# Turning the unit maxima in a fused attention and dense block: a TensorE product against VectorE block transposes

## The chip, the cores and the metric

One Trainium2 chip, one of its cores. A core has five engines that run side by side, each through its own queue in order: TensorE (PE in the profile, its weight loads PEld), VectorE (DVE), ScalarE (ACT), GpSimd (POOL) and SyncE (SP), which here only issues DMAs. The metric is the device time of one launch in microseconds; a comparison takes the median over several runs.

## What is computed

`x` is 2048 rows of 512 numbers, all float32. The result is `x + s * g`:

```python
xn = _layernorm(x, axis=-1)
# s: attention with 32 heads of 16 channels over the 2048 rows
q, k, v = split(xn @ wqkv)
scores = einsum("bhqd,bhkd->bhqk", q, k) * (16 ** -0.5)
s = einsum("bhqk,bhkd->bhqd", softmax(scores), v).reshape(B, S, D) @ wo
# g: a dense block
g = silu(gelu(xn @ w1 + b1) @ w2 + b2)
out = x + s * g
```

For the softmax the kernel takes the largest score of every query row and head away ahead of the exponential. That maximum has to be known before the exponentials of that row start, so the kernel computes the scores twice: once with the queries along the partitions, to take the maximum, and once with the keys along the partitions, for the exponentials.

## The kernel before

**Units.** The attention is cut into 32 units: unit `u` is a group of 4 heads (`u // 4`) and a chunk of 512 queries (`u % 4`). Products in nearly full precision are made from a high and a low part of each operand (float32r, "hi" and "lo").

**Two stages.** In the first, up to about 470 us of the span, TensorE works through the dense block (`mm`, line 583: products of half the array's height, 64 rows, which run two at a time, one on each row tile, `a` = 0 or 1). Between them `fill` (line 561) puts score products for the maxima, one for each 5 products of the dense block (`APART`), 576 in all, which is units 0 to 8. In the second stage, the loop over `n` at line 976 runs 512 steps. Each step has four transposed score products with their exponentials (`t_one`, line 708: TensorE, then ScalarE), the four products with the values (`pv_step`, line 775, the row of line 781) and three score products for the maxima of units further ahead (`s_op`, line 209). The order inside a step is written out by hand (`ORDER`, `AFTER`).

**Banks.** Results of TensorE go to PSUM banks. In stage one the score products for the maxima take turns on two banks (`s_tile`: `ps_a`, `ps_b`), in stage two on three (`ps_x` joins). The transposed scores take turns on four banks (`t_tile`, line 700: `ps_m` and three of `ps_t`). A product waits until the reader of the bank's earlier content is done.

**Maxima of a unit.** `s_max` (line 188) reduces every score product on VectorE, 512 columns to two maxima (line 191, 2048 times). When the 64 products of a unit are done:

- `s_end0` (line 238): VectorE reduces what is left to 16 columns, negated, `nm` (line 248); GpSimd rounds it to a high part and takes the low part (lines 251 and 252) into `nmh`. Queries lie along the partitions, 128 at a time; the 16 columns are 4 heads by 4 query blocks.
- The second score product wants each head's maxima as two rows along the queries (high and low), which are multiplied with rows of ones. So the columns have to be turned into rows. Units 0 to 27 go through this in pairs, the last four one by one (`units_of`).
- `s_end1` (line 265), some products later: one TensorE product of `nmh` (up to 64 columns) with the identity `ident_r`. Its bank is one of the score ring in stage one, one of the four of `t_tile` in stage two, and one of the score ring for the last unit. In `fill` it takes the slot of a score product (line 565 to 570).
- `s_end2` (line 271): the bank is copied to `mh`, by ScalarE in stage one (line 276) and by VectorE in stage two (line 278), and one DMA on SP stores it to `mh_d` in HBM, rows of 128 numbers (line 279).
- `load_mh` (line 150): two DMAs on SP read `mh_d` into rows 48 and 49, and 112 and 113, of the queries of `t_one` (`QT`), at steps fixed ahead of time.

SP's queue is in order and holds also the loads of queries (line 136), of weights (line 292) and the moves of results (lines 801 to 814).

Of the kernel before, what the change touches and what calls it, by code (L numbers as in the profile page):

```python
# [8 lines left out]
F32 = mybir.dt.float32  # L9
F32R = mybir.dt.float32r  # L10
AF = mybir.ActivationFunctionType
OP = mybir.AluOpType
AX = mybir.AxisListType
# [3 lines left out]
P = 128  # L17
# [6 lines left out]
CH = 512  # L24
NCH = S // CH
F = 1376
FT = (F + P - 1) // P
GH = 4
NG = H // GH
# [7 lines left out]
FILL0 = 30  # L37
APART = 5
# [12 lines left out]
def fused(ctx: ExitStack, tc: tile.TileContext, x, wqk, wv, wo, w1, b1, w2, b2, out):  # L51
    nc = tc.nc
    ctx.enter_context(tc.manual_schedule())
    dpool = ctx.enter_context(tc.tile_pool(name="scratch", bufs=1, space=DRAM))
    keep = ctx.enter_context(tc.tile_pool(name="keep", bufs=1))
# [9 lines left out]
    ones_d = dpool.tile([2, S], F32, name="ones_d")  # L65
    g_d = dpool.tile([S, D], F32, name="g_d")
    den_d = dpool.tile([NG * NCH, GH, CH], F32, name="den_d")
    mh_d = dpool.tile([NG * NCH, 2, GH, CH], F32, name="mh_d")

    ident_r = keep.tile([P, P], F32R, name="ident_r")  # L70
    mhw = keep.tile([1, 1], F32, name="mhw")
    vsb = keep.tile([P, NT, H * VW + DH], F32, name="vsb")
    kts, kws, qts, qzs = [], [], [], []
# [10 lines left out]
            if then:  # L84
                then()

    QS, QT, MX, NM, MH = {}, {}, {}, {}, {}
    SYNC = mybir.DependencyInfo(mybir.DependencyClass.Sync, mybir.DependencyReason.DATA)
    qss = []
    NU = NG * NCH  # L90
# [3 lines left out]
    def s_tile(held=False):  # L94
        pool = s_ring.pop(0)
        if not held:
            s_ring.append(pool)
        return pool.tile([P, CH], F32, name="ps"), pool
# [22 lines left out]
    def new_k(pool):  # L121
        both = pool.tile([P, 2, S], F32R, name=f"kt{len(kts)}")
        kws.append(both)
        kts.append([both[:, p] for p in range(2)])
# [13 lines left out]
    def load_qs(u, sides=range(2)):  # L138
        if u < NU:
            QS[u] = qzs[u % 2] if u < LEAD // 16 else qss[0][:, u % 2]  # L140
            q_rows(QS[u], u, sides)

    def ask_qs(u):
        errands[:0] = [(load_qs, u, (a,)) for a in range(2)]
# [5 lines left out]
    def load_mh(u):  # L150
        assert u in sent
        for a in range(2):
            nc.sync.dma_start(QT[u][64 * a + 48:64 * a + 50].bitcast(F32), mh_d[u, :, a::2, :])

    heads = [(u, st, p) for u in range(NU) for st in range(NCH * NCH) for p in range(2)]
    made = [0, 0]
    done = {u: 0 for u in range(NU)}
    later, ended, errands, sent = [], [], [], set()

    def units_of(u):  # L160
        return (u,) if u >= PAIRED else (u - u % 2, u - u % 2 + 1)

    def tick():
        for e in later:
            e[0] -= 1

    def flush():
        while later and later[0][0] <= 0:
            u = later.pop(0)[1]
            run_off()  # L170
            s_end1(u)
            s_end2(u)

    def at_of(job):
        u, st, p = job
# [27 lines left out]
    def s_one(a):  # L203
        made[a] += 1
        s_whole(heads[made[a] - 1], a)
# [28 lines left out]
    def run_off():  # L234
        while put_off:
            put_off.pop(0)()

    def s_end0(u):
        ended.remove(u)
        nm = qring.tile([P, GH * NCH], F32, name="nm")  # L240
        n = len(units_of(u))
        if u == units_of(u)[0]:
            NM[u] = qring.tile([P, 2, 2, GH * NCH], F32R, name="nmh")[:, :n]
        hl = NM[units_of(u)[0]][:, u % n]
        if u == units_of(u)[-1]:
            later.append([12 if "seen" in prog else 8, units_of(u)[0]])
        mx = MX.pop(u).rearrange("p a b c n -> p (a b) (c n)")
        nc.vector.tensor_reduce(nm, mx, axis=AX.X, op=OP.max, negate=True)  # L248

        def two():  # L250
            nc.gpsimd.tensor_copy(hl[:, 0], nm)  # L251
            nc.gpsimd.tensor_sub(hl[:, 1], nm, hl[:, 0].bitcast(F32))

        put_off.append(two)
        if "seen" in prog or u == NU - 1:
            run_off()
        del QS[u]
        if "seen" in prog:
            ask_qs(u + 2)
        else:  # L260
            load_qs(u + 2)

    prog = {}

    def s_end1(u):
        pm = s_tile()[0] if "seen" in prog or u == NU - 1 else t_tile()
        n = 2 * GH * NCH * len(units_of(u))
        nc.tensor.matmul(pm[:n, :P], NM.pop(u).rearrange("p u i a -> p (u i a)"), ident_r, start=True, stop=True)
        MH[u] = pm

    def s_end2(u):
        us = units_of(u)
        n = 2 * GH * NCH * len(us)
        mh = qring.tile([4 * GH * NCH, P], F32, name="mh", bufs=1)
        if "seen" in prog:
            nc.scalar.activation(mh[:n], MH.pop(u)[:n, :P], AF.Copy)
        else:
            nc.vector.tensor_copy(mh[:n], MH.pop(u)[:n, :P])
        nc.sync.dma_start(mh_d[us[0]:us[-1] + 1].rearrange("u i j (q s) -> (u i j q) s", s=P), mh[:n])
        sent.update(us)  # L280

    sa = ExitStack()
# [4 lines left out]
    b1_sb = xp.tile([P, FT], F32, name="b1_sb")  # L287
# [26 lines left out]
    for j in range(len(pairs)):  # L314
        for h in range(2):
# [4 lines left out]
            due = next((i for i in range(j, len(pairs)) if is_m[i]), len(pairs))  # L320
# [4 lines left out]
            n = 2 if nd < len(parts) and parts[nd][2] and ready - nd > room else 1  # L325
            n = max(n, need - 2 * (left - 1))
            while nd < ready and n > 0:
                c, f, k = parts[nd]
# [63 lines left out]
    with ExitStack() as s1:  # L392
# [18 lines left out]
        ident = wp.tile([P, P], F32, name="ident")  # L411
# [68 lines left out]
        def consts():  # L480
            one = w1k.tile([2, 1, P // 2], F32, name="one", bufs=1)
            nc.gpsimd.memset(one, 1.0)
            nc.gpsimd.dma_start(ones_d.rearrange("r (n c) -> r n c", c=P // 2),
                                one.to_broadcast([2, 2 * NT, P // 2]))
            nc.gpsimd.tensor_copy(ident_r, ident)
            nc.gpsimd.dma_start(b1_sb, b1)
            nc.gpsimd.dma_start(b2_sb, b2.rearrange("(o d) -> o d", o=1).to_broadcast([P, D]))

# [50 lines left out]
    keep_r = ctx.enter_context(tc.tile_pool(name="keep_r", bufs=1, side="right"))  # L539
    qring = ctx.enter_context(tc.tile_pool(name="qring", bufs=2, side="right"))  # L540
    new_k(keep_r)
    kts.append([kv[:, p] for p in range(2)])
    kws.append(kv)
    qts.append(keep_r.tile([P, 2, CH], F32R, name="qt0"))
# [12 lines left out]

    prog.update(n=0, pe=0, seen=0)
    writer = {}
    s_when, put, row = [], [0], [0]  # L560
    def fill(a):
        due = 2 * FILL0 + APART * (put[0] + sum(made))
        if sum(made) < 4 * LEAD and row[0] >= due and (made[0] <= made[1]) == (a == 0):
            taken()
            if later and later[0][0] <= 0:
                put[0] += 1
                u = later.pop(0)[1]
                s_end1(u)
                s_end2(u)
                return  # L570
            whole_units = list(ended)
            s_one(a)
            for u in whole_units:
                s_end0(u)
            tick()

    def taken():
        prog["pe"] += 1
        s_when.append(prog["pe"])
        if len(s_when) > 2:  # L580
            prog["seen"] = max(prog["seen"], s_when[-3])
# [86 lines left out]
    def half(j, h):  # L668
        x, y = pairs[j]
        if h == 0:  # L670
            PH[x] = ps_x.tile([P, CH], F32, name="ps")
            PH[y] = ps_m.tile([P, CH], F32, name="ps")
            run((terms(x, 0, True), terms(y, 1, True)), {4: [lambda: w1_split(j + 1)], 8: [errand], 10: [chore]})
        else:
            run((terms(y, 0, False), terms(x, 1, False)), {2: [lambda: w1_load(j + 2), errand], 10: [chore]})
            evac((x, y), PH)
# [23 lines left out]
    def t_tile():  # L700
        turns[0] += 1
        if turns[0] < 5:
            pool = (ps_m, ps_x, ps_a, ps_b)[turns[0] - 1]
        else:
            pool = ps_m if turns[0] % 4 == 1 else ps_t
        return pool.tile([P, CH], F32, name="pst" if pool is ps_t else "ps")
# [13 lines left out]
    for n, e in enumerate(plan):  # L720
        if e[0] == "half":
            half(*e[1:])
        elif e[0] == "first":
            quad(*e[1:])
            if e[1:] == (0, 2):
                ask_qs(1)
        else:
            if e[1] == parts[-2]:
                nc.scalar.activation(mhw, ident_r[:1, :1].bitcast(F32), AF.Exp)
            if e[1] == parts[-1]:  # L730
                for i in range(EARLY):
                    t_one(0, 0, i // 2, i % 2)
            down(*e[1])
        if e == ("first", VQ - 1, 2):
            w2_split(0)
            w2_load(2)
            ask_k(1)
        if e[0] == "half" and pairs[e[1]][0] == ("q", NG - 1, 0) and e[2] == 1:
            kts.append([slot(p, (P, S), F32R) for p in range(2)])
            kws.append(None)  # L740
            qss.append(slot(2, (P, 2, 2, CH), F32R))
            ask_k(2)
        if n == len(plan) - 8:
            load_qt(0)
            load_mh(0)
# [207 lines left out]
    for t in range(NW):  # L953
        n = DONE + 4 * (t // 2)
# [9 lines left out]
    for i, t in enumerate(late):  # L964
        n = L - 2 * len(late) - 1 + 2 * i
# [10 lines left out]
    for n in range(L + 1):  # L976
        ua, ka = divmod(n, 16)
        want = due(n) - due(n - 1)
        i = 0
# [75 lines left out]
```

## Time and profile before

| what | us |
|---|---|
| median of 3 runs | 1565.8 (1565.47 to 1566.19) |
| profiled execution, its own time | 1565.5 |
| its span, first to last instruction | 1563.7 |
| PE busy | 1556.6 (100% of the span) |
| DVE busy | 1416.1 (91%) |
| ACT busy | 1234.5 (79%) |
| POOL busy | 371.7 (24%) |
| granted TensorE clock | 1.00 throughout |

How to read the rows that follow: a row of a timeline has the start in us from the start of the span, the length in us, engine, line of the kernel, operation, what is written and read, shapes, and how many were merged; in brackets the idle time of the engine ahead of it and what ended that. Operations of one engine may overlap, since they are pipelined, and ends of products are modelled. A row of a group or tile has the count behind the x and the durations in ns (least, median, greatest, or one mean). A row of the stretches has the engines' busy us with the number of their instructions in brackets.

### The profile page before, as it was taken

What the parts mean: (1) busy time and instruction counts of PE and PEld (TensorE: products, weight loads), DVE (VectorE), ACT (ScalarE), POOL (GpSimd) and SP (SyncE); (2) the same over time, 40 slices, a digit from 0 to 9 for tenths busy, and PEclk for the clock granted to TensorE, in tenths of its full rate; (3) what the DMA queues carried; (4) which work ended last, traced back from release to release, by engine and by line L of the source; (5) the groups of instructions that cost most, each with busy time, mean ns of one, the idle gap of its engine ahead of it and who ended that gap; (6) DMA issues with size and microseconds to landing.
All of it is one profiled execution on the core that took longest, in us unless ns stands there. A gap on an engine that the chain in (4) does not pass through costs nothing.

```text
span 1563.7 us, 31870 instructions
## 1 busy us (share of the span) xinstructions
PE 1556.6 (100%) x12264; PEld 951.5 (61%) x12264; DVE 1416.1 (91%) x2290; ACT 1234.5 (79%) x2397; POOL 371.7 (24%) x394
## 2 busy tenths in 40 slices
PE   9999999999999999999999999999999999999998
PEld 7899999999994444444444444444444444444455
DVE  7599999999999999999999999999999999999834
ACT  4333333434349999999999999999999999999984
POOL 4145575756640011001100100100010000000143
PEclk9999999999999999999999999999999999999999
DMA  6626343454322113111511411321151111110163
GB/s 209 153 60 158 116 139 100 155 145 136 124 91 60 40 42 61 29 38 44 86 24 28 70 41 32 59 44 29 26 79 27 33 29 33 40 30 22 46 197 115
DMA packets 74648, 116.87 MB, mean 75 GB/s; under 512 B 23013, under 2 KB 24293, under 8 KB 73321
## 3 DMA queue, kind: packets, MB, share of 16 engines
q1 hardware_dynamic: 70748, 101.89, 23.9%
q0 software_dynamic: 3264, 12.35, 4.7%
q8 instruction: 97, 1.59, 0.4%
q10 hardware_dynamic: 484, 0.60, 0.1%
q14 instruction: 55, 0.44, 0.1%
HBM read 84.35 MB, written 25.97 MB: 71 GB/s over the span
## 4 chain that ended last, share of the span: by engine, by line
PE 98%; DVE 1%; ACT 0%; DMA 0%; issue 0%; DVEq 0%
PE pv L781 33%; PE pst L715 20%; PE ps L589 13%; PE ps L185 11%; PE pst L589 7%; PE ps L715 7%; PE pv L589 2%; PE ps L905 1%; PE ps L82 1%; PE ps L459 1%; PE pst L82 1%; DVE st L418 0%; PE pst L441 0%; DMA xt<-in_x 0%; PE pst L459 0%; ACT slot L717 0%
## 5 line engine op out<-in xcount | busy, mean ns | idle before, releaser
L191 DVE TENSOR_REDUCE mx<-ps 128x2 f32<-128x512 f32 x2048 | 1317.9, 687 | 87.2 <-PE ps L185 44.4
L717 ACT ACTIVATE slot<-pst 128x512 f32<-128x512 f32 x1533 | 826.0, 603 | 12.8 <-PE pst L715 7.0
L781 PE MATMUL pv<-slot,vsb 128*32 128x512 f32 x4096 | 545.4, 605 | 0.3 <-DVE os L788 0.3
L715 PE MATMUL pst<-qt,kt 50*128 50x512 f32 x1149 | 378.8, 430 | 0.5 <-DVE gt L648 0.3
L185 PE MATMUL ps<-kt,slot 48*128 48x512 f32 (+1 forms) x1364 | 377.1, 368 | 0.0
L715 PEld LDWEIGHTS pst<-qt,kt 50*128 50x128 f32 x1149 | 192.3, 185 | 252.5 <-ACT slot L717 235.9
L717 ACT ACTIVATE slot<-ps 128x512 f32<-128x512 f32 x515 | 310.9, 604 | 1.8 <-PE ps L185 0.7
L185 PEld LDWEIGHTS ps<-kt,slot 48*128 48x128 f32 x1364 | 226.6, 184 | 39.4 <-DVE mx L191 35.4
L589 PE MATMUL ps<-slot,w1h 64*128 64x512 f32 x1088 | 218.4, 393 | 0.0
L185 PE MATMUL ps<-kt,qz 48*128 48x512 f32 x512 | 201.8, 394 | 0.0
L185 PE MATMUL ps<-slot,slot 48*128 48x512 f32 (+1 forms) x598 | 165.3, 366 | 0.0
L715 PE MATMUL ps<-qt,kt 50*128 50x512 f32 x387 | 160.6, 417 | 0.0
L589 PEld LDWEIGHTS ps<-slot,w1h 64*128 64x128 f32 x1088 | 151.9, 186 | 10.5
L589 PE MATMUL ps<-slot,w1l 64*128 64x512 f32 x544 | 148.4, 393 | 0.0
L781 PEld LDWEIGHTS pv<-slot,vsb 128*32 128x32 f32 x4096 | 81.0, 108 | 98.9 <-issue 90.4
L378 POOL TENSOR_TENSOR hl<-hg,hh 128x512 fp32r<-128x512 f32 x76 | 96.8, 1296 | 151.9 <-ACT hh L377 113.9
L251 POOL CAST nmh<-nm 128x16 fp32r<-128x16 f32 x32 | 6.3, 197 | 519.4 <-DVE nm L248 418.0
L371 ACT ACTIVATE hg<-ps,b_sb 128x512 f32<-128x512 f32 x44 | 27.9, 684 | 125.2 <-PE ps L589 100.4
L715 PE MATMUL pst<-qt,slot 50*128 50x512 f32 x384 | 112.5, 416 | 0.0
L185 PEld LDWEIGHTS ps<-slot,slot 48*128 48x128 f32 x598 | 99.1, 184 | 16.4 <-DVE mx L191 15.1
L715 PEld LDWEIGHTS ps<-qt,kt 50*128 50x128 f32 x387 | 71.3, 185 | 41.8 <-ACT slot L717 36.0
L185 PEld LDWEIGHTS ps<-kt,qz 48*128 48x128 f32 x512 | 94.0, 184 | 0.5
(165 smaller groups left out, 1722.6 us busy)
## 6 DMA issues: line engine op xcount, KB each, us to landing
raw<-in_w SPq DMA_DIRECT2D x88, 256.0 KB
qk_h<-hh SPq DMA_DIRECT2D x32, 256.0 KB
qk_l<-hl SPq DMA_DIRECT2D x32, 256.0 KB
qt<-qk_h SPq DMA_DIRECT2D x128, 64.0 KB
slot<-qk_h SPq DMA_DIRECT2D x92, 64.0 KB
g_d<-gt POOLq DMA_DIRECT2D x16, 256.0 KB, 3.4
qt<-qk_l SPq DMA_DIRECT2D x64, 64.0 KB
dn<-den_d SPq DMA_DIRECT2D x32, 128.0 KB
```

Source lines behind the costliest of these rows:

```text
L82: nc.tensor.matmul(ps, lhs[a], rhs[b], start=first and n == 0, stop=last and n == 2)
L185: return nc.tensor.matmul(ps[:, c0:c0 + w], QS[u][r, p, qi * P:(qi + 1) * P], kts[u // NCH % KB][p][r, k0:k0 + w], start=True, stop=True).ins
L191: nc.vector.tensor_reduce(MX[u][:, 2 * p:2 * p + 2, qi, ki][:, heads, parts], ps.rearrange("p (n c) -> p n c", c=HC), axis=AX.X, op=OP.max)
L251: nc.gpsimd.tensor_copy(hl[:, 0], nm)
L371: nc.scalar.activation(raw, ph.pop(u), AF.Gelu_apprx_tanh, bias=b1_sb[:, u[2]:u[2] + 1])
L378: nc.gpsimd.tensor_sub(hl, raw, hh.bitcast(F32))
L459: nc.tensor.matmul(pq["q", g, c], W1[g][i][:, k * P:(k + 1) * P], (xh, xl)[j][c][:, k], start=n == 0 and k == 0, stop=n == 2 and k == KT - 1)
L589: i = nc.tensor.matmul(ps, lhs[r], rhs[r], start=first, stop=last).ins
L715: nc.tensor.matmul(ps, kts[g % KB][p][r, k * P:(k + 1) * P], QT[u][r, p, :], start=True, stop=True)
L717: nc.scalar.activation(PT[u, k][:, 2 * p + a, :], ps, AF.Exp, scale=SCALE)
L781: nc.tensor.matmul(PV[u][32 * j:32 * j + 32, :], vsb[:, k, h:h + 32], PT[u, k][:, j, :], start=(k == 0), stop=(k == NT - 1))
L905: HALF[0] = nc.tensor.matmul(PW[i][0], OTS[i, k][x][r], (wo_h, wo_l)[y][r, k], start=k == 0 and side == 0 and n == 0, stop=k == KT - 1 and ...
```

## The change

The unit maxima are turned by VectorE instead of TensorE. VectorE's transpose turns squares of 32 by 32 numbers, each in its place, so a tile of 128 partitions and 32 columns (a pair of units) becomes four squares, one under the other: partition `32 b + m`, column `s` then holds column `m` of query `32 b + s`. GpSimd splits this turned tile into high and low part, and four DMAs, one for each `b`, store it in runs of 32 numbers into the places that the rows of 128 had. `mh_d` has high and low part as its first index now. The reduce of a unit writes one half of a tile of 32 columns that two pairs share by turns (`nms`, set to zero once).

Gone are the TensorE product, its bank, the copy from it, the identity in float32r, and the slot that `fill` gave to it. GpSimd works once for a pair instead of once for a unit.

```diff
-    mh_d = dpool.tile([NG * NCH, 2, GH, CH], F32, name="mh_d")
-    ident_r = keep.tile([P, P], F32R, name="ident_r")
+    mh_d = dpool.tile([2, NG * NCH, GH, CH], F32, name="mh_d")
...
-            nc.sync.dma_start(QT[u][64 * a + 48:64 * a + 50].bitcast(F32), mh_d[u, :, a::2, :])
+            nc.sync.dma_start(QT[u][64 * a + 48:64 * a + 50].bitcast(F32), mh_d[:, u, a::2, :])
...
     def s_end0(u):
         ended.remove(u)
-        nm = qring.tile([P, GH * NCH], F32, name="nm")
-        n = len(units_of(u))
-        if u == units_of(u)[0]:
-            NM[u] = qring.tile([P, 2, 2, GH * NCH], F32R, name="nmh")[:, :n]
-        hl = NM[units_of(u)[0]][:, u % n]
-        if u == units_of(u)[-1]:
-            later.append([12 if "seen" in prog else 8, units_of(u)[0]])
+        us = units_of(u)
+        w = u % 2 * GH * NCH
+        nm = nms[u // 2 % 2]
         mx = MX.pop(u).rearrange("p a b c n -> p (a b) (c n)")
-        nc.vector.tensor_reduce(nm, mx, axis=AX.X, op=OP.max, negate=True)
+        nc.vector.tensor_reduce(nm[:, w:w + GH * NCH], mx, axis=AX.X, op=OP.max, negate=True)
+        if u == us[-1]:
+            later.append([12 if "seen" in prog else 8, us[0]])
+            nt = qring.tile([P, 2 * GH * NCH], F32, name="nt")
+            nc.vector.transpose(nt, nm)
+            mh = MH[us[0]] = qring.tile([P, 2, 2 * GH * NCH], F32R, name="mh")

         def two():
-            nc.gpsimd.tensor_copy(hl[:, 0], nm)
-            nc.gpsimd.tensor_sub(hl[:, 1], nm, hl[:, 0].bitcast(F32))
+            if u == us[-1]:
+                nc.gpsimd.tensor_copy(mh[:, 0], nt)
+                nc.gpsimd.tensor_sub(mh[:, 1], nt, mh[:, 0].bitcast(F32))
...
-    def s_end1(u):
-        pm = s_tile()[0] if "seen" in prog or u == NU - 1 else t_tile()
-        n = 2 * GH * NCH * len(units_of(u))
-        nc.tensor.matmul(pm[:n, :P], NM.pop(u).rearrange("p u i a -> p (u i a)"), ident_r, start=True, stop=True)
-        MH[u] = pm
-
-    def s_end2(u):
+    def s_send(u):
         us = units_of(u)
-        n = 2 * GH * NCH * len(us)
-        mh = qring.tile([4 * GH * NCH, P], F32, name="mh", bufs=1)
-        if "seen" in prog:
-            nc.scalar.activation(mh[:n], MH.pop(u)[:n, :P], AF.Copy)
-        else:
-            nc.vector.tensor_copy(mh[:n], MH.pop(u)[:n, :P])
-        nc.sync.dma_start(mh_d[us[0]:us[-1] + 1].rearrange("u i j (q s) -> (u i j q) s", s=P), mh[:n])
+        mh = MH.pop(u)
+        n = GH * NCH
+        for b in range(4):
+            r0 = 32 * b + u % 2 * n
+            dst = mh_d[:, us[0]:us[-1] + 1].rearrange("i u j (q b s) -> b (u j q) i s", q=NCH, b=4)[b]
+            nc.sync.dma_start(dst, mh[r0:r0 + n * len(us)].bitcast(F32))
         sent.update(us)
...
+    nms = [qring.tile([P, 2 * GH * NCH], F32, name=f"nm{i}", bufs=1) for i in range(2)]
+    for nm in nms:
+        nc.gpsimd.memset(nm, 0.0)
...
-    s_when, put, row = [], [0], [0]
+    s_when, row = [], [0]
     def fill(a):
-        due = 2 * FILL0 + APART * (put[0] + sum(made))
+        due = 2 * FILL0 + APART * sum(made)
...
             if later and later[0][0] <= 0:
-                put[0] += 1
-                u = later.pop(0)[1]
-                s_end1(u)
-                s_end2(u)
-                return
+                s_send(later.pop(0)[1])
...
-                nc.scalar.activation(mhw, ident_r[:1, :1].bitcast(F32), AF.Exp)
+                nc.scalar.activation(mhw, b1_sb[:1, :1], AF.Exp)
```

In the order of the instructions, PE lists the same as before without the 18 products. On VectorE a transpose follows the small reduce of each pair's second unit, and of each of the last four units. On SP four stores stand at the place of each single one. On ScalarE four copies are gone.

More of the change, by code (lines that the diff above doesn't have):

```diff
@@ L85, in mm3 @@
                 then()
-    QS, QT, MX, NM, MH = {}, {}, {}, {}, {}
+    QS, QT, MX, MH = {}, {}, {}, {}
     SYNC = mybir.DependencyInfo(mybir.DependencyClass.Sync, mybir.DependencyReason.DATA)
@@ L170, in flush @@
             run_off()
-            s_end1(u)
-            s_end2(u)
+            s_send(u)
     def at_of(job):
@@ L484, in consts @@
                                 one.to_broadcast([2, 2 * NT, P // 2]))
-            nc.gpsimd.tensor_copy(ident_r, ident)
             nc.gpsimd.dma_start(b1_sb, b1)
@@ L565, in fill @@
             if later and later[0][0] <= 0:
-                put[0] += 1
-                u = later.pop(0)[1]
-                s_end1(u)
-                s_end2(u)
-                return
+                s_send(later.pop(0)[1])
             whole_units = list(ended)
```

## The prediction

> **What bounds the kernel now.** I read the stretches of the span first, because the program has two stages that have nothing in common but TensorE; then the groups, for the tiles that the change touches; then the order of time around one such place in each stage.
>
> ```profile
> PE 1556.6 (100%) x12264; PEld 951.5 (61%) x12264; DVE 1416.1 (91%) x2290; ACT 1234.5 (79%) x2397; POOL 371.7 (24%) x394
> 200.00:300.00 100.00, 100.00 (x857) 94.31 (x855) 96.22 (x145) 37.28 (x68) 65.61 (x59) 1.00 0.40 128
> 700.00:800.00 100.00, 100.00 (x781) 47.47 (x785) 94.21 (x156) 99.20 (x195) 13.33 (x19) 1.00 0.31 54
> ```
>
> The columns of the second and third row are PE, PEld, DVE, ACT and POOL busy, the granted clock, the DMA share, GB/s. In the first stage (the dense block, with score products put between its products) PE starts 857 products in 100 us, 0.117 us each, two row tiles side by side: a PE bound, with VectorE 3.8 us short of full. In the second stage (exponentials, value products, the rest of the score products) ScalarE is busy 99.20 of 100 us, and PE waits for it bank by bank. So in stage one a thing costs what it takes of PE; in stage two it costs only if ScalarE is left without a finished bank.
>
> ```profile
> L268 PE MATMUL ps<-ident_r,nmh x9: 248/275/275, 156.7 to 1482.5; 128*64 128x128 f32 x7, 128*32 128x128 f32 x2
> L268 PE MATMUL pst<-ident_r,nmh x9: 247/275/277, 611.4 to 1397.1; 128*64 128x128 f32 x7, 128*32 128x128 f32 x2
> L278 DVE COPY mh<-pst x9: 270/272/283, 611.7 to 1397.4; 64x128 f32<-64x128 f32 x7, 32x128 f32<-32x128 f32 x2
> L248 DVE TENSOR_REDUCE nm<-mx x32: 273/276/288, 104.4 to 1479.9; 128x16 f32<-128x128 f32 x32
> ```
>
> The work that goes is 18 products with the identity (14 pairs of units, 4 single units). By the code four lie in stage one, with a ScalarE copy each; fourteen in stage two, with a VectorE copy of 0.27 us each. Eighteen times 0.275 is 5 us of PE, but what counts is how long the others stood still.
>
> **Removed in stage one: four products.** Here is one of the four, PE in order of time.
>
> ```profile
> 428.75 0.39 PE L589 MATMUL ps<-slot,w1h 64*128 64x512 f32 x1
> 429.07 0.28 PE L268 MATMUL ps<-ident_r,nmh 128*64 128x128 f32 x1
> 429.27 0.50 PE L589 MATMUL ps<-slot,w1h 64*128 64x512 f32 x2
> 429.62 0.39 PE L589 MATMUL ps<-slot,w1l 64*128 64x512 f32 x2
> 429.85 0.39 PE L185 MATMUL ps<-slot,qz 48*128 48x512 f32 x1
> ```
>
> From 428.75 to 429.85 five half-height products start (one, two, two); at 0.117 us each they need 0.58 us, and they take 1.10. The full-height product costs 0.51 us, since both row tiles run empty before it and start together after it. The other three are the same form at the same kind of place; I take them alike: 4 x 0.51 = 2.0 us gained. The ScalarE copy there has cover (ScalarE is 37% busy). The slot that line 566 gave to it falls to a score product, so later ones come up to 20 rows earlier; that moves work, and takes none away.
>
> **Removed in stage two: fourteen products, their bank and copy.** The beat is the distance between starts of value products (line 781), one per step.
>
> ```profile
> 608.38 1.07 PE L781 MATMUL pv<-slot,vsb 128*32 128x512 f32 x8
> 610.41 1.07 PE L781 MATMUL pv<-slot,vsb 128*32 128x512 f32 x8
> 611.40 0.28 PE L268 MATMUL pst<-ident_r,nmh 128*64 128x128 f32 x1
> 612.14 1.09 ACT L717 ACTIVATE slot<-pst 128x512 f32<-128x512 f32 x2 [0.16 <-PE ps L185]
> 612.68 0.64 PE L781 MATMUL pv<-slot,vsb 128*32 128x512 f32 x4
> 1439.23 1.06 PE L781 MATMUL pv<-slot,vsb 128*32 128x512 f32 x8
> 1441.50 1.07 PE L781 MATMUL pv<-slot,vsb 128*32 128x512 f32 x8
> 1443.51 1.06 PE L781 MATMUL pv<-slot,vsb 128*32 128x512 f32 x8
> ```
>
> The step with the product takes 2.27 us in both (610.41 to 612.68, 1439.23 to 1441.50); its neighbours take 2.03 and 2.01. The product takes a turn of the bank ring that the exponentials use, the next score bank is 0.2 us late, and ScalarE shows the hole (0.16). These two are an early and a late one of the fourteen; with 0.24 us for thirteen and 0.2 for the last, which stands among output products, that is 3.3 us gained. The gain asked for at most is so 2.0 + 3.3 = **5.3 us**.
>
> **Added: eighteen turns on VectorE.** No row shows such a turn. Nearest is a VectorE operation on 128 rows with 16 numbers each; a far upper end is one that reads 512.
>
> ```profile
> L809 DVE RECIPROCAL dr<-dr 128x16 f32<-128x16 f32 x32 | 7.8, 243 | 3.4 <-DMA dr<-os 3.4
> L191 DVE TENSOR_REDUCE mx<-ps 128x2 f32<-128x512 f32 x2048 | 1317.9, 687 | 87.2 <-PE ps L185 44.4 <-PE pst L715 3.9 <-PE ps L715 1.8
> ```
>
> I take 0.24 us (32 numbers are nearer to 16 than to 512), with 0.69 as the dear end; the cheap end is 0, where it hides wholly. It reads what the reduce just ahead of it writes, so it can't overlap that one as the next score reduce does now:
>
> ```profile
> 149.07 0.28 DVE L248 TENSOR_REDUCE nm<-mx 128x16 f32<-128x128 f32 x1
> 149.26 4.09 DVE L191 TENSOR_REDUCE mx<-ps 128x2 f32<-128x512 f32 x6
> 60.00:440.00 380.00, 365.31 (x537) 1.00 0.43 124
> L185 PE MATMUL ps<-kt,qz 48*128 48x512 f32 x512 | 201.8, 394 | 0.0
> ```
>
> The third row is line 191 alone in stage one. Today the small reduce delays the next score reduce by 0.19 us. With the turn it is 0.28 + 0.24, less some overlap at its end: about 0.27 more. The cover: 380 us over 537 reduces is one score product per 0.708 us, with two banks; two periods (1.42) less the product (0.39) and its reduce (0.69) leave 0.33, of which 0.19 is used already. So 0.27 meets 0.14, and PE would stand about 0.15 us at each of the four: **0.6 us lost** in stage one (nothing at the cheap end; at 0.69, 0.6 us each, 2.4).
>
> In stage two VectorE has 5.8 us of idle time in 100, and score products have a third bank. Two things of known size are put between the score reduces there already: the small reduce and, once a unit, a copy of 512.
>
> ```profile
> 607.67 0.28 DVE L248 TENSOR_REDUCE nm<-mx 128x16 f32<-128x128 f32 x1
> 601.34 0.68 DVE L788 COPY os<-pv 128x512 f32<-128x512 f32 x1
> 602.11 1.06 PE L781 MATMUL pv<-slot,vsb 128*32 128x512 f32 x8
> 604.30 1.07 PE L781 MATMUL pv<-slot,vsb 128*32 128x512 f32 x8
> ```
>
> The small one costs nothing (608.38 to 610.41 after it is a plain 2.03); the copy of 0.68 is followed by a step of 2.19, 0.15 too long. A reduce and a turn, 0.52 together, lie between: 0 to 0.1, taken as 0.05 for each of thirteen, **0.65 us lost**; the last stands where VectorE is idle. At the dear end (0.28 + 0.69) it is up to 0.5 each, 6.5 us. The VectorE copies that go pay for the turns in busy time, in another step; their cost is already in the 0.24.
>
> The Trainium skill, "VectorE: DVE Perf Modes", The three transpose paths, gives 311 ns to a VectorE turn and 390 ns to a TensorE one, both of 128x128 bf16; by that an estimate of the sum with 0.31 in place of 0.24 loses some 0.07 us more at 17 places, about 1 us, and no row here has a turn to hold against it.
>
> **Added: stores.** SP issues four stores where it issued one, 54 more in all, each of 64 runs (32 for single units) of 128 bytes. Rows for the last unit, the one with the least time:
>
> ```profile
> 1484.94 0.33 SPq L279 DMA_DIRECT2D mh_d<-mh  x1
> 1486.38 1.36 SPq L153 DMA_DIRECT2D qt<-mh_d  x2
> 1491.86 0.49 PE L715 MATMUL pst<-qt,kt 50*128 50x512 f32 x1
> 1480.55 0.22 POOL L252 TENSOR_TENSOR nmh<-nm,nmh 128x16 fp32r<-128x16 f32 x1
> ```
>
> Now: Pool is done at 1480.77, but product, bank and copy hold the store until 1484.94; it lands within 1.44 us, the loads are issued by 1487.74, their first reader starts at 1491.86, 4.1 us later. Afterwards Pool is done about 0.3 us later (the turn ahead of it), and the four stores, 0.33 to 0.53 us of SP each, can be out by about 1483.2: before the single one is issued today. SP's other loads move by some 1.5 us at eighteen places and have more room than that. Cost 0, the cover being those 4.1 us and the 1.7 won ahead of them. Pool has 18 pairs of small operations instead of 32, and two fills of 32 numbers at the start, before its queue matters: 0.
>
> **The sum.** Against the profiled execution's own 1565.5 us (span 1563.7 and 1.8 around it; 0.3 below the median 1565.8): 1565.5 - 2.0 - 3.3 + 0.6 + 0.65 = 1561.45; brought to the median by the 0.3, **1561.7 us**, 0.26% down. A measurement here can tell about 0.2%, 3.1 us, from no change, so below 1562.7 counts as faster.
>
> **Rivals.** *VectorE gives most of it back.* The turn takes 0.4 to 0.5 us with its waits: 0.3 to 0.4 lost at each of four, 0.2 at each of thirteen, some 4 of the 5.3 us; 1563 to 1566. For it: VectorE is 94 to 96% busy in both stages, and the turn is bound to the reduce ahead of it. Against: operations on few numbers take 0.16 to 0.28 us here.
>
> *The turn is a long operation: slower.* Some VectorE forms of this kernel take 1 us:
>
> ```profile
> L843 DVE SCALAR_TENSOR_TENSOR gx<-slot,gx 128x512 f32<-128x512 f32 x10 | 10.2, 1016 | 17.8 <-ACT slot L842 13.8 <-POOL gx L916 4.0
> ```
>
> At 1.0 us, stage one loses 1.03 - 0.14 = 0.9 at four places and stage two about 0.8 at thirteen: 14 against 5.3 gained, 1574. It decides from about 0.55 us for the turn (even), and is 3 us slower from about 0.75. For it: nothing shows the form. Against: 1 us is for 512 numbers in two inputs, not 32.
>
> *The stores land late.* The Trainium skill, "DMA: Bandwidth & Descriptors", Specifications, puts the least transfer for full rate at 512 bytes, with a read and write back below; these runs are of 128. As a mechanism of this kernel: the last unit's loads wait for all four landings, and the first scores of that unit wait for the loads; landing 5 us later than today costs nothing, 12 us later costs 7 less the 4 gained, 1569. Against: even four stores in a row, each issued after the last has landed (0.53 + 1.44 us), are done at 1489 and just in time. Other units have more room than the last.
>
> *All of it is clean*, nothing lost to VectorE: 1565.8 - 5.3 = 1560.5, or a little less where the products cost more than I took.
>
> **Chances.** My forecast 0.66 (own range 1560.3 to 1563.2; 0.58 of it below 1562.7, 0.08 above); clean or better 0.04; VectorE gives most back 0.18; long turn 0.08; late stores 0.04. Faster 0.62, same 0.26, slower 0.12. The range, 1559.8 to 1566.0, holds the forecast, the clean case and VectorE giving most back; outside are the two slow cases and some edges, under 0.2.
>
> **What would show it.** In stage one, the place of the four products without the 0.51 us gap, and about 858 products per 100 us there; VectorE's turn near 0.24 us, and after it score products late by 0.15 at most. In stage two, plain steps of 2.03 to 2.06 where 2.27 stood, ScalarE without the 0.16 hole. At the last unit, loads issued before 1486 and the first scores not waiting. I am wrong if the turn is above 0.4 us, if steps with it lengthen by over 0.1, or if PE's waits for line 191 grow in stage one.

## The result, and the profile after

| what | before | changed |
|---|---|---|
| median, us | 1565.93 (1565.47 to 1566.44) | 1563.45 (1563.23 to 1564.40) |
| ratio | | 0.9985, 95% interval 0.9978 to 0.9992 |
| profiled execution, us | 1565.5 | 1564.16 |
| its span, us | 1563.7 | 1562.4 |

The kernel is 2.5 us faster, 0.15%, where 4.1 was forecast (1565.8 to 1561.7, 0.26%). The time lies in the range of 1559.8 to 1566.0 and on the side that was forecast. But it lies under the bound of 0.2%, where the prediction put 0.62 on more than that, and 0.25 us outside the forecast's own range of 1560.3 to 1563.2.

The first thing to ask is in which stage the missing part went. The value products start with the second stage and end with it, so one row of each kernel, all records of that line with their first and last start, cuts the span. Before:

```profile
L781 PE MATMUL pv<-slot,vsb x4096: 592/593/619, 470.4 to 1541.8; 128*32 128x512 f32 x196
```

The changed kernel:

```profile
L772 PE MATMUL pv<-slot,vsb x4096: 592/593/618, 469.4 to 1540.5; 128*32 128x512 f32 x196
```

The first stage is 1.0 us shorter (470.4 to 469.4), and the second, from first to last value product, 1071.1 instead of 1071.4. So in the second stage, where by the forecast 3.3 us were taken away, all but 0.3 came back.

The new operations, all records of their tiles in the changed kernel (count, then ns least, median, greatest):

```profile
L246 DVE STREAM_TRANSPOSE nt<-nm x18: 211/211/214, 149.7 to 1479.0; 128x32 f32<-128x32 f32 x18
L251 POOL CAST mh<-nt x18: 205/209/211, 150.0 to 1479.3; 128x32 fp32r<-128x32 f32 x18
```

The turn takes 0.21 us. It isn't a long operation. VectorE in order of time, at one place of the second stage of the changed kernel:

```profile
1132.56 0.28 DVE L242 TENSOR_REDUCE nm<-mx 128x16 f32<-128x128 f32 x1
1132.94 0.21 DVE L246 STREAM_TRANSPOSE nt<-nm 128x32 f32<-128x32 f32 x1
1133.08 3.73 DVE L189 TENSOR_REDUCE mx<-ps 128x2 f32<-128x512 f32 x6
```

and TensorE at the same place:

```profile
1131.21 1.07 PE L772 MATMUL pv<-slot,vsb 128*32 128x512 f32 x8
1133.27 1.07 PE L772 MATMUL pv<-slot,vsb 128*32 128x512 f32 x8
1134.26 0.50 PE L706 MATMUL ps<-qt,slot 50*128 50x512 f32 x1
...
1134.72 0.39 PE L706 MATMUL pst<-qt,slot 50*128 50x512 f32 x1
1134.98 0.50 PE L183 MATMUL ps<-kt,slot 48*128 48x512 f32 x1
1134.98 0.50 PE L706 MATMUL pst<-qt,slot 50*128 50x512 f32 x1
1135.32 0.28 PE L183 MATMUL ps<-kt,slot 48*128 48x256 f32 x1
1135.53 1.07 PE L772 MATMUL pv<-slot,vsb 128*32 128x512 f32 x8
1137.54 1.04 PE L772 MATMUL pv<-slot,vsb 128*32 128x512 f32 x5
```

The reader is to see three things. The step where the old product stood, two behind the small reduce, is now a plain one: 1135.53 to 1137.54 is 2.01. The step right behind the small reduce, plain before, now takes 2.26 (1133.27 to 1135.53). And its delay sits at one point: the second whole score product of that step starts at 1134.98, 0.26 after the product ahead of it, because it waits for a reduce to give its bank back, the third of the merged row that starts at 1133.08. That reduce by itself:

```profile
1134.24 0.68 DVE L189 TENSOR_REDUCE mx<-ps 128x2 f32<-128x512 f32 x1
```

It ends at 1134.92, and the product starts 0.06 us behind that. Before, the same three reduces started 0.23 us behind the small reduce (607.67, 607.90), here 0.52. While the product waits, both row tiles run empty and start together again (0.50 us for each, not 0.39), and what PE has behind it in order, the fourth transposed score product, the last score half and the value products, is late. At the other places of the second stage, but for the last unit's, the step behind the turn takes 2.18 to 2.26 (2.18 and 2.19 at the two where the reduces go on 0.45 behind the small reduce and not 0.52). For the units 28 and 29 it takes 2.39 and 2.52, and there it was long before already, 2.16 and 2.30.

In the first stage of the changed kernel the same pair of instructions meets two banks instead of three; VectorE, and then TensorE, in order of time:

```profile
149.37 0.28 DVE L242 TENSOR_REDUCE nm<-mx 128x16 f32<-128x128 f32 x1
149.68 0.21 DVE L246 STREAM_TRANSPOSE nt<-nm 128x32 f32<-128x32 f32 x1
149.82 1.93 DVE L189 TENSOR_REDUCE mx<-ps 128x2 f32<-128x512 f32 x3
```

```profile
150.35 0.39 PE L580 MATMUL ps<-slot,w1h 64*128 64x512 f32 x1
150.52 0.50 PE L183 MATMUL ps<-kt,qz 48*128 48x512 f32 x1
150.58 0.67 PE L580 MATMUL ps<-slot,w1h 64*128 64x512 f32 x2
```

The score reduces go on 0.45 us behind the small reduce (0.19 before), the score product at 150.52 waits for the first of them, which by itself is this row:

```profile
149.82 0.65 DVE L189 TENSOR_REDUCE mx<-ps 128x2 f32<-128x512 f32 x1
```

It ends at 150.47, 0.05 us ahead of the product, and the dense block behind the product waits too. The waits of TensorE's weight loads between 60 and 455 us (total, times, longest), before and then in the changed kernel, show this wait as new:

```profile
PEld ps L268 <- issue: 1.4, 4, 0.4
PEld ps L183 <- DVE mx L189: 0.8, 3, 0.3
```

The stores, SP's queue in the changed kernel at the last unit:

```profile
1479.87 1.89 SPq L272 DMA_DIRECT2D mh_d<-mh  x4
1482.82 0.53 SPq L152 DMA_DIRECT2D qt<-mh_d  x2
```

The four stores are issued by 1481.76 and have landed by 1482.82, when the loads are issued, 3.6 us earlier than before.

### The profile page after: what moved, and what is told of

The parts are those of the page before. It is cut to its first block, busy times and chain, and to the rows that moved or that the text cites. A ratio compares the mean times of both kernels' runs of the same rounds, so it can differ in the third digit from the quotient of the medians.

```text
span 1562.4 us, 31826 instructions
## 1 busy us (share of the span) xinstructions
PE 1555.6 (100%) x12246; PEld 955.1 (61%) x12246; DVE 1414.8 (91%) x2294; ACT 1232.5 (79%) x2393; POOL 366.8 (23%) x367
## 4 chain that ended last, share of the span: by engine, by line
PE 97%; DVE 1%; DMA 1%; ACT 0%; issue 0%; DVEq 0%
PE pv L772 33%; PE pst L706 14%; PE ps L580 13%; PE ps L706 12%; PE ps L183 12%; PE pst L580 7%; PE pv L580 2%; PE ps L896 1%; PE ps L452 1%; PE ps L81 1%; PE pst L81 0%; DVE st L411 0%; DMA dn<-den_d 0%; DMA xt<-in_x 0%; PE pst L434 0%; DMA dr<-os 0%
## 5 line engine op out<-in xcount | busy, mean ns | idle before, releaser
L708 ACT ACTIVATE slot<-pst 128x512 f32<-128x512 f32 x1533 | 803.9, 606 | 0.6 <-PE ps L706 0.6
L708 ACT ACTIVATE slot<-ps 128x512 f32<-128x512 f32 x515 | 307.5, 598 | 13.7 <-PE ps L706 6.2
L706 PE MATMUL pst<-qt,kt 50*128 50x512 f32 x1149 | 307.0, 403 | 0.4 <-DVE gt L639 0.3
L580 PE MATMUL ps<-slot,w1h 64*128 64x512 f32 x1088 | 226.0, 392 | 0.0
L706 PEld LDWEIGHTS pst<-qt,kt 50*128 50x128 f32 x1149 | 208.1, 185 | 19.3 <-DVE gt L639 1.0
L706 PE MATMUL ps<-qt,kt 50*128 50x512 f32 x387 | 190.8, 495 | 0.0
L580 PEld LDWEIGHTS ps<-slot,w1h 64*128 64x128 f32 x1088 | 155.8, 185 | 7.9
L580 PE MATMUL ps<-slot,w1l 64*128 64x512 f32 x544 | 159.5, 392 | 0.0
L706 PE MATMUL pst<-qt,slot 50*128 50x512 f32 x384 | 100.5, 404 | 0.0
L810 POOL TENSOR_TENSOR ot<-ot,dn 64x512 f32<-64x512 f32 x15 | 19.2, 1280 | 301.1 <-DMA dn<-den_d 257.6
```

The lines of the kernel that those rows point to most:

```text
L580: i = nc.tensor.matmul(ps, lhs[r], rhs[r], start=first, stop=last).ins
L706: nc.tensor.matmul(ps, kts[g % KB][p][r, k * P:(k + 1) * P], QT[u][r, p, :], start=True, stop=True)
L708: nc.scalar.activation(PT[u, k][:, 2 * p + a, :], ps, AF.Exp, scale=SCALE)
L810: eng.tensor_mul(ot[c][rs, g // 2], ot[c][rs, g // 2], DN.pop(u)[rs])
```

## The experiments

The rows above suggest one theory, **A, place:** the turn right behind the reduce makes VectorE late by more than the banks cover. Two others stand against it. **B, form:** the transpose as such hinders other engines. **C, stores:** the 54 more stores of short runs eat the gain. All kernels below are compared with the kernel before, run on the same chip (medians 1565.74 for the first four, 1565.87 for the others).

**No turn.**

```diff
-            nt = qring.tile([P, 2 * GH * NCH], F32, name="nt")
-            nc.vector.transpose(nt, nm)
+            nt = nm
...
-                nc.scalar.activation(raw, ph.pop(u), AF.Copy)
+                nc.scalar.activation(raw, ph.pop(u), AF.Copy, scale=0.125)
```

> The changed kernel without VectorE's eighteen turns: GpSimd splits the small reduce's tile as it lies, so that the maxima stand in the wrong places; the queries and keys are made 8 times smaller each, so that this does no harm. Theory A (VectorE's time at one place: the reduce and the turn behind it make the score reduces 0.45 us late instead of 0.2, the score banks come late, 0.2 us lost at each of four places in stage one and of fourteen in stage two, two of these 0.36 and 0.48): all of it comes back, 0.9 + 3.2, so 1559.4 against 1563.45. Rival B (the turn as a form of instruction hinders other engines, wherever it stands): the same here. Rival C (the four stores and their 128-byte runs eat the gain): no change, 1563.4.

Measured: 1560.37 us, ratio 0.9966 (0.9953 to 0.9978). The turns' price is so 3.1 us, and the stores, still there, are not it. C falls. A and B expected 1.0 us less time than this; they took the price from the changed kernel's profiled execution, which lies 0.7 above its median.

**The turn later.** Only the place of the turn, and of what follows it, is changed: a list `owed`, counted down by score products and by quarters of a step, as `later` is.

```diff
-            nc.vector.transpose(nt, nm)
...
+            owed.append([0 if u == NU - 1 else 6 if "seen" in prog else 8, two])
...
         def two():
+            nt = qring.tile([P, 2 * GH * NCH], F32, name="nt")
+            nc.vector.transpose(nt, nm)
```

> The turn is taken away from the small reduce: it comes six score products later in stage one and at the end of the second step after in stage two, with GpSimd's split behind it and the stores one step later; the last unit stays as it is. Same instructions. Theory A: by then VectorE has caught up, a turn alone is shorter than the small reduce, which costs nothing: about 1559.5 to 1560.5, and the steps behind a reduce fall from 2.25 to 2.03. Rival B: the loss moves with the turn, 1563.4, steps of 2.25 where the turn now stands. Rival C: 1563.4.

Measured: 1559.90 us, ratio 0.9964 (0.9951 to 0.9976), as without any turn. VectorE and the starts of the value products in this kernel:

```profile
868.01 0.28 DVE L249 TENSOR_REDUCE nm<-mx 128x16 f32<-128x128 f32 x1
868.24 1.89 DVE L196 TENSOR_REDUCE mx<-ps 128x2 f32<-128x512 f32 x3
870.28 1.89 DVE L196 TENSOR_REDUCE mx<-ps 128x2 f32<-128x512 f32 x3
872.08 0.20 DVE L252 STREAM_TRANSPOSE nt<-nm 128x32 f32<-128x32 f32 x1
872.31 1.29 DVE L196 TENSOR_REDUCE mx<-ps 128x2 f32<-128x512 f32 x2
```

```profile
866.68 1.07 PE L779 MATMUL pv<-slot,vsb 128*32 128x512 f32 x8
868.72 1.06 PE L779 MATMUL pv<-slot,vsb 128*32 128x512 f32 x8
870.75 1.06 PE L779 MATMUL pv<-slot,vsb 128*32 128x512 f32 x8
872.79 0.64 PE L779 MATMUL pv<-slot,vsb 128*32 128x512 f32 x4
```

With the reduce alone the steps are 2.04, 2.03 and 2.04, and the step behind the turn, 872.79 to 874.82, takes 2.03. The same eighteen turns, at a time when VectorE isn't late already, cost nothing that can be seen. B falls.

**The turn twice.**

```diff
             nc.vector.transpose(nt, nm)
+            n2 = qring.tile([P, 2 * GH * NCH], F32, name="n2")
+            nc.vector.transpose(n2, nm)
```

> Each turn is made twice, the second into a tile that nobody reads. Theory A: with no slack left after the first, the second one's 0.14 to 0.21 us is lost in full at eighteen places: 2.5 to 3.8 more, 1566.0 to 1567.2. Rival B: twice the loss, 1567.4. Rival C: no change, 1563.4.

Measured: 1565.42 us, ratio 0.9997 (0.9988 to 1.0006): 2.0 us more than the changed kernel, below what was expected. VectorE's rows, and below them the starts of the value products, say why: the second turn reads what is ready long since and holds the next reduce up by only 0.09 us.

```profile
1133.75 0.28 DVE L242 TENSOR_REDUCE nm<-mx 128x16 f32<-128x128 f32 x1
1134.13 0.21 DVE L246 STREAM_TRANSPOSE nt<-nm 128x32 f32<-128x32 f32 x1
1134.27 0.17 DVE L248 STREAM_TRANSPOSE n<-nm 128x32 f32<-128x32 f32 x1
1134.36 1.85 DVE L189 TENSOR_REDUCE mx<-ps 128x2 f32<-128x512 f32 x3
```

```profile
1134.46 1.06 PE L774 MATMUL pv<-slot,vsb 128*32 128x512 f32 x8
1136.81 1.07 PE L774 MATMUL pv<-slot,vsb 128*32 128x512 f32 x8
```

The step takes 2.35, which is 0.09 more than with one turn, and at the other twelve places of the second stage whose step the turn lengthens it is 0.08 to 0.10 more too, but for one with 0.33: past the cover, VectorE's lateness goes on to the step one for one.

**A copy in place of the turn.**

```diff
-            nc.vector.transpose(nt, nm)
+            nc.vector.tensor_copy(nt, nm)
...
-                nc.scalar.activation(raw, ph.pop(u), AF.Copy)
+                nc.scalar.activation(raw, ph.pop(u), AF.Copy, scale=0.125)
```

> A plain VectorE copy of the same 128 by 32 numbers stands in place of the turn, so the maxima stand in the wrong places; queries and keys are 8 times smaller as in the run without a turn. Theory A: a copy takes about as long as the turn (0.2 us) and costs the same, 1563.0 to 1563.6. Rival B (it is the form): the loss goes, 1559.5 to 1560. Rival C: 1563.4.

Measured: 1563.69 us, ratio 0.9988 (0.9979 to 0.9996), 0.1 above what A expected.

```profile
L246 DVE COPY nt<-nm x18: 181/182/183, 149.6 to 1478.7; 128x32 f32<-128x32 f32 x18
```

So it is not the form: a plain copy that waits for the same reduce costs what the turn costs. Together with the turn taken later, which is free, this leaves the place as the cause.

**One order for all steps.** The prediction had taken the copy of a unit's values, 0.68 us on VectorE for a step only 0.15 too long, as proof of cover. But two steps beside that copy have orders of their own in the code: the one that ends with the value products the copy waits for (step 0 of the next unit), and the one in which the copy's lateness shows (step 2).

```diff
-AFTER = {0: "STXTTSTYV", 2: "XTSTTYSTV"}
+AFTER = {}
```

> The changed kernel with the one default order in every step of three score products: the hand-written orders of steps 0 and 2 of each unit, which follow the copy of a finished unit's values (0.68 us on VectorE), are left out. Theory A says that VectorE has about 0.25 us of cover in a plain step; then the copy, 0.6 us late, is only as cheap as 0.15 because of those two orders, and without them each of thirty costs 0.3 to 0.4: 4.5 to 7.5 more, 1568 to 1571. Rival D (the copy is cheap because VectorE's lateness has more cover, and the turns are dear for another reason): within 1 us of 1563.45.

Measured: 1567.90 us, ratio 1.0013 (1.0004 to 1.0022): 4.45 more than the changed kernel, 0.15 for each of thirty copies, and 0.1 below the range that A expected. Starts of the value products around one copy, in this kernel:

```profile
700.36 1.06 PE L772 MATMUL pv<-slot,vsb 128*32 128x512 f32 x8
702.70 1.06 PE L772 MATMUL pv<-slot,vsb 128*32 128x512 f32 x8
```

The step is 2.34 long with the default order, 2.19 with the written one (602.11 to 604.30 before). In a default step the copy's lateness of 0.60 costs 0.30, at the low end of what was expected, and the 0.52 of reduce and turn cost 0.22. Both leave about 0.30 that is covered, of which the small reduce alone takes 0.23. Rival D falls; the yardstick was taken from steps that had been arranged for it.

**The stores twice, on the kernel with the turn later.**

```diff
             nc.sync.dma_start(dst, mh[r0:r0 + n * len(us)].bitcast(F32))
+            dst = mh_e[:, us[0]:us[-1] + 1].rearrange("i u j (q b s) -> b (u j q) i s", q=NCH, b=4)[b]
+            nc.sync.dma_start(dst, mh[r0:r0 + n * len(us)].bitcast(F32))
```

> The kernel with the turn taken later (1559.9), and each of the 72 stores made a second time into a second scratch tensor that nobody reads. Theory A: stores have cover, 1559.7 to 1560.3. Rival C: the stores' share shows again, 1561 or more.

Measured: 1560.71 us (1559.63 to 1561.19), ratio 0.9965 (0.9953 to 0.9978) against 0.9964 with single stores. The median is above what A expected and below what C expected, and the runs scatter more than those of the other kernels; by the ratios to their own kernels before, the two can't be told apart. In the profiled execution the first value product starts at 469.2 where it is 468.6 with single stores, and TensorE waits once in the first stage, 0.5 us, for a weight part that GpSimd makes, as it does in the kernel without a turn (0.7 us); whether the stores had a part in it wasn't tried. A cost of some tenths of a microsecond stays open.

**The product back, on the kernel with the turn later.**

```diff
         mh = MH.pop(u)
+        pm = s_tile()[0] if "seen" in prog or u == NU - 1 else t_tile()
+        nc.tensor.matmul(pm[:4 * GH * NCH, :P], mh.rearrange("p i a -> p (i a)"), ident_r, start=True, stop=True)
```

> The kernel with the turn taken later (1559.9), and at each place of the stores the old TensorE product with the identity, into a bank of the same rings as before; no copy, and nobody reads it. It takes no slot of a score product. If the price of what was removed is the product with its turn of the bank ring (0.51 us at four places, 0.24 at fourteen), 5.3 comes back: 1564.7 to 1565.6. If the copy, or the slot, was the larger part: 1562 or less.

Measured: 1565.63 us, ratio 0.9997 (0.9989 to 1.0006): nothing that can be told from noise is left of the 5.8 us by which the kernel with the turn later is faster. One place:

```profile
785.31 1.06 PE L783 MATMUL pv<-slot,vsb 128*32 128x512 f32 x8
786.31 0.28 PE L276 MATMUL pst<-ident_r,mh 128*64 128x128 f32 x1
787.57 1.06 PE L783 MATMUL pv<-slot,vsb 128*32 128x512 f32 x8
```

The step takes 2.26 us without any copy from the bank, as it did before the change. The cut of this kernel shows both gains gone, 470.6 for the first value product and 1071.1 from it to the last:

```profile
L783 PE MATMUL pv<-slot,vsb x4096: 592/593/618, 470.6 to 1541.7; 128*32 128x512 f32 x196
```

So the price lay in the product with its turn of the ring; the copies, and the slot in `fill`, were no part of it that can be seen. How it divides between the product itself and the bank wasn't tried.

**The turn a little later only.**

```diff
-            owed.append([0 if u == NU - 1 else 6 if "seen" in prog else 8, two])
+            owed.append([0 if u == NU - 1 else 2 if "seen" in prog else 4, two])
```

> The turn comes two score products behind the small reduce in stage one (six in the run with the turn later), and at the end of the same step in stage two (end of the second step there); stores as in the changed kernel. Theory A: three score reduces lie between, the wait for the reduce's result is gone and VectorE has caught up by most of the 0.2: no loss or up to 0.05 at a place, 1559.8 to 1560.8. If the lateness needs longer to die out: 1561 to 1563.

Measured: 1559.86 us, ratio 0.9961 (0.9949 to 0.9974). So two score products in stage one, and the end of the same step in stage two, are distance enough. This version and the one with the longer distance are the fastest measured, 0.39 and 0.36% below the kernel before.

## Why the prediction was right, and where it was not

The cut at the value products gives each term its own measurement, from one profiled execution of each kernel. The kernel with the turn later has both gains without the price of the turn:

```profile
L779 PE MATMUL pv<-slot,vsb x4096: 592/593/618, 468.6 to 1536.7; 128*32 128x512 f32 x196
```

- **Stage one, four products, 2.0 us:** right. 470.4 to 468.6 is 1.8, and with the product back the first value product starts at 470.6.
- **Stage two, fourteen products, 3.3 us:** right. 1071.4 falls to 1068.1, which is 3.3, and putting the product alone back restores it.
- **The turn's length, 0.24, and VectorE's added lateness, 0.27:** right. The turn takes 0.211 us, and the score reduces go on 0.45 to 0.52 behind the small reduce instead of 0.19 in stage one, and 0.29 later at the place of stage two shown above. The 311 ns that the Trainium skill (VectorE: DVE Perf Modes, The three transpose paths) gives is for a larger form, which no run here shows; the smaller one took 0.21.
- **Lost in stage one, 0.15 at each of four, 0.6:** a little small. 469.4 less 468.6 is 0.8, and the new waits of the weight loads for the score reduces are 0.8 too.
- **Lost in stage two, "0 to 0.1, taken as 0.05 for each of thirteen, 0.65 us lost":** this is the step that failed. It cost 0.16 to 0.25 at each of thirteen places, against the same step before, and 1071.1 less 1068.1 = 3.0 us together. The interpolation between a free reduce of 0.28 and a copy of 0.68 that cost 0.15 used a row whose steps had another order of products. In a default step the small reduce had used 0.23 of the cover of about 0.30, so that most of what came behind it was lost. Two of the prediction's own signs of being wrong came true with it: steps with the turn lengthened by over 0.1, and PE's waits for the score reduces grew in stage one, from none to 0.8 us.
- **Stores and GpSimd, 0:** right within what the runs tell, some tenths of a microsecond; the stores of the last unit land earlier than before, not later. The rule of the Trainium skill on short runs (DMA: Bandwidth & Descriptors, Specifications) decides nothing here: at the last unit, four stores of 128-byte runs had landed within 1.1 us of the last issue.

With 3.0 in place of 0.65 and 0.8 in place of 0.6, the prediction's own sum for a profiled execution is 1565.5 - 5.3 + 3.8 = 1564.0. The one of the changed kernel, from which these sizes are, took 1564.16; it lies 0.7 above the median of 1563.45, and what that execution had more than the others isn't known. By the medians the turns cost less than the 3.8: 3.1 to 3.6 us, the changed kernel against those without a turn and with the turn later. Of the prediction's rivals, the one in which VectorE gives most of it back (1563 to 1566) is what happened, by the cover and not by a longer turn; that the time still lies in the range is so because the range held this rival too.

## What to carry to other kernels

Before a known operation is used as a yardstick for a new one, look whether the order around it was arranged to bear it; its price holds for its place only. Where an engine is nearly full, a dependent pair put back to back costs its wait as well as its work: put the second half a few operations later, and both may be free. And a change that moves work from one engine to another is best read with the span cut by stage: here both gains were whole, and one stage gave its gain back.

## What was not expected of the hardware

A VectorE operation that reads what the one ahead of it writes started 0.31 to 0.39 us behind the start of a reduce of 0.28, where an independent one mostly starts 0.19 to 0.27 behind; a second turn on data that was ready held VectorE for only 0.09 us, though each is shown as 0.17 to 0.21 long. At the two places shown above, about half of the lateness that the turn adds (0.26 and 0.29 us) is so this wait. And one product of full height among products of half height cost the four places of stage one about 0.5 us each (470.4 and 470.6 with it, 468.6 without), nearly twice its own 0.275.
